# Talking-heads attention and Fourier mixing on one core: the Fourier transform folded a second time, and the second pair of row groups laid out about row 224

## The chip, the cores and the metric

The kernel runs on one core of a Trainium2 chip. The core has TensorE (matrix products, called PE in the profile, with PEld for its weight loads), VectorE (DVE), ScalarE (ACT), GpSimd (POOL) and SyncE (SP, which here only issues transfers). All five run their own queues in order and meet at semaphores. The metric is the device time of one execution in microseconds; several executions are timed and the median is given.

## What is computed

The reference joins two blocks. `x` is the attention result with its heads side by side, and it feeds a Fourier mixing layer with a feed-forward part. All numbers are fp32 (the two feed-forward weights come as 64-bit floats).

```python
batch, n_heads, seq, head_dim = (8, 12, 448, 64)
scores = scale * np.matmul(q, k.transpose(0, 1, 3, 2))
scores = np.einsum('bhij,hg->bgij', scores, w_pre)        # pre-mix of the heads
attn = softmax(scores)
attn = np.einsum('bhij,hg->bgij', attn, w_post)           # post-mix
x = np.matmul(attn, v)                                    # to (8, 448, 768)

X = np.fft.fft(x, axis=1)
X = np.fft.fft(X, axis=2)
u = x + np.real(X)
un = (u - mean(u)) / np.sqrt(var(u) + 1e-06)
out = u + np.maximum(un @ w_ch1, 0.0) @ w_ch2             # 768 -> 3072 -> 768
```

The real part of the two-dimensional transform is a sum of two products: cosines along the rows times cosines along the columns, less sines times sines. Cosines are even and sines odd, so rows `s` and `448 - s` may be added (or subtracted) before the product with cosines (or sines), and columns `d` and `768 - d` likewise. That is a fold: half as many rows and columns go into the products.

## The kernel before, in words

There are two phases. `mix_phase` does attention and the Fourier transform and leaves `u` in DRAM (`u_scr`). `ffn_phase` reads it and does the normalization and the feed-forward part. The change touches only the first.

**Steps.** The first phase runs through 192 steps, 24 for each of 8 batches, and is written as a software pipeline in one loop. A step handles 10 query rows of all heads twice over. Its stages lie in different steps: at step `s` the gather (`emit_gather`, SP) collects the scores of step `s + 4`; the pre-mix (`emit_premix`, L425, TensorE), the row maximum (`emit_max`, L433, DVE), the exponential (`emit_exp`, L441, ScalarE) and the scaling by the reciprocal sum (`emit_scale`, L449 and L450 on DVE, L452 on GpSimd) belong to step `s + 2`; the post-mix (`emit_postmix`, L462, TensorE) and the 32x32 transposes of its result (`emit_turn`, L473, DVE) belong to step `s`. The pre-mix writes the PSUM tile `mx`, of which there is one; the post-mix writes `po`, also one.

**Other work.** Between these stages work of four kinds is taken from lists by due time, counted in steps from the batch's first: score matmuls (`emit_qk`, L399, due times `AT_QK`), products of attention and values (`emit_av`, L489, `AT_AV`), transposes of q and k (`emit_xpose`, L376, `AT_T`), and the Fourier part below. Their results lie in four PSUM tiles (`pms`, tile `ms`). Their evictions from PSUM (`copy`, L285) wait in a list, `pend`, and are emitted by `flush`; the table `ENG` says which go to ScalarE ("a") and which to DVE ("d"). One operation on the feed-forward weights (`wts.deal(1)`) is added to DVE in each step.

**Row groups.** A batch's 448 rows form four groups of 112. Groups 0 and 1 hold rows 0 to 111 and their mirror images 447 down to 337, stored in reverse with one zero row. Groups 2 and 3 hold rows 112 to 224 and their mirror images 336 down to 225. `emit_av` writes a group transposed into `XT`; in a backward group (`back`) it writes with a negative step, and a memset (L513) clears the row without a partner. `emit_x` (L525, due at `AT_X`) transposes it to `X` (rows on partitions). After each second group `fold` puts six GpSimd operations into a list: sums of the two groups in two halves (L547), the fold of the columns (L551, L552), differences in two halves (L547) and their fold (L557). They give `xe` (385 columns) and `xo` (383). One of them is emitted in each step.

**Transform.** `emit_z` (L570, `AT_Z`) multiplies 97 to 128 columns of `xe` (or `xo`) of both row pairs with the row table `ts` (225 frequencies) and gives one of seven tiles `z`. `emit_s2` (L584, `AT_S`) multiplies the four even (or three odd) `z` with the column tables `tce` or `tdo` (385 frequencies), for one pair of row groups at a time. DVE adds the result to `X` and its mirror image (L595, L597). Then the rows go to `u_scr`: the forward group by SP (L610, and L612 for row 224), the backward group by an indirect transfer that GpSimd issues (L604).

**Order.** The order of TensorE, DVE and ScalarE is the order written in the loop (`manual_schedule`). The order of GpSimd's and SP's queues is set by the framework's scheduler when the program is built.

Of the kernel before, what the change touches and what calls it, by code (L numbers as in the profile page):

```python
# [16 lines left out]
P = 128  # L17
# [10 lines left out]

R = 5
# [9 lines left out]
PR = (GR, GR + 1)  # L39
XW = GR + 12  # L40
# [11 lines left out]

SH = S // 2
DH = DM // 2
EVEN = [(0, 97), (97, 96), (193, 96), (289, 96)]
ODD = [(0, 128), (128, 128), (256, 127)]
# [6 lines left out]
AT_T = ((7, 0), (18, 18), (15, 17))  # L63
AT_QK = ((0, 2, 2), (0, 1, 2), (0, 1, 2), (0, 1, 2),
         (0, 1, 2), (1, 1, 2), (0, 1, 2), (0, 1, 2))
AT_AV = ((0, 2, 4), (0, 1, 4), (3, 4, 5), (2, 3, 4))
AT_X = (11, 20, 25, 29)
AT_Z = (38, 38, 38, 38, 42, 42, 42)
AT_S = ((41, 44), (49, 53))

ENG = {("tr", "q", 4): "d", ("tr", "q", 3): "a", ("tr", "k", 4): "a",
       ("tr", "k", 3): "d", "QK": "aa", "AV": "aa", "X": "aa", "z": "a"}

# [9 lines left out]
def _consts():  # L83
    s = np.arange(S)
    ang = 2.0 * np.pi * (np.outer(s, np.arange(SH + 1)) % S) / S
    ts = np.zeros((GR + 1, 2, 2, SH + 1))
    for n in range(2):
        for x, fn in enumerate((np.cos, np.sin)):
            ts[:PR[n], n, x] = fn(ang[n * GR:n * GR + PR[n]])
    d = np.arange(DH + 1)  # L90
    ang = 2.0 * np.pi * (np.outer(d, d) % DM) / DM
    tc = np.zeros((P, len(EVEN), DH + 1))
    for n, (d0, w) in enumerate(EVEN):
        tc[:w, n] = np.cos(ang[d0:d0 + w])
    td = np.zeros((P, len(ODD), DH + 1))
    for n, (d0, w) in enumerate(ODD):
        td[:w, n] = np.sin(ang[d0 + 1:d0 + 1 + w])
# [3 lines left out]
    for x in range(2):  # L101
        for r in range(R):
# [4 lines left out]
    at = S - GR * np.arange(2) - np.arange(GR)[:, None]  # L107
    return {"at": at.astype(np.uint32), "ts": ts.astype(np.float32),
            "tc": tc.astype(np.float32), "td": td.astype(np.float32),
            "mk": mk.astype(np.float32)}  # L110
# [142 lines left out]
def mix_phase(ctx, tc, ident, q, k, v, w_pre, w_post, u_scr, wts):  # L253
# [19 lines left out]
    pxf = pool("pxf", 2)  # L273
# [49 lines left out]
    rows = cst.tile([GR, 2], U32, name="rows")  # L323
    ts = cst.tile([GR + 1, 2, 2, SH + 1], F32, name="ts")
    tce = cst.tile([P, len(EVEN), DH + 1], F32, name="tce")
    tdo = cst.tile([P, len(ODD), DH + 1], F32, name="tdo")

    def emit_tables():
        for t, n in ((rows, "at"), (ts, "ts"), (tce, "tc"), (tdo, "td")):
            nc.sync.dma_start(out=t, in_=cn[n].ap())  # L330
        return []
# [343 lines left out]
    with tc.manual_schedule(engines={ET.PE, ET.DVE, ET.Activation}):  # L675
        while s < TOT or any(fill.values()):
# [5 lines left out]
            if 0 <= s + LM < TOT:  # L682
                emit_exp(s + LM)
# [306 lines left out]
```

## Time and profile before

| What | Value |
|---|---|
| Median of three executions | 2539.23 us (2535.92 to 2539.9) |
| Profiled execution | 2539.07 us, span 2537.3 us |
| Mean granted TensorE clock | 0.989 |
| Busy: PE, DVE, ACT, POOL | 95%, 59%, 31%, 27% of the span |
| Last post-mix to first feed-forward matmul | 905.65 to 964.10 us |
| A batch in the steady stretch (first `z` to first `z`) | 107.9 to 110.4 us |

The first phase takes the first 15 of the 40 slices of the page. There the other engines are busier than the shares of the whole span say: from 542.81 to 651.50 us DVE works 82.7 of 108.7 us, ScalarE 70.6 and GpSimd 68.6. In lines of the timeline the first number is the start and the second the time to the last end, in microseconds; the bracket tells how long the engine was idle before and what it waited for. Consecutive matmuls overlap, so the pace is read from start to start.

### The profile page before, as it was taken

Reading aid. Unit: us, or ns where it says so; the run is one execution under the profiler, and the core shown is the slowest. Engines: PE = TensorE matmul, PEld = TensorE weight load, DVE = VectorE, ACT = ScalarE, POOL = GpSimd, SP = SyncE. Lnnn points to the kernel's source line nnn. Section 1 sums busy time; section 2 is a strip of 40 time slices with the busy share of each in tenths; the row PEclk is TensorE's granted clock in tenths of the full one; section 3 lists DMA queues with packets and bytes.
Section 4 is the critical chain, followed back from the end, with each engine's and each line's share of the span. In section 5 each row is a group of like instructions: output and inputs, shape, how many; then the busy total and the mean of one; then the engine's idle time right before and its main releaser. Section 6 shows DMA issues by size and latency. Waiting matters only on the chain.

```text
span 2537.3 us, 47605 instructions
## 1 busy us (share of the span) xinstructions
PE 2418.7 (95%) x18544; PEld 1555.7 (61%) x18544; DVE 1503.3 (59%) x3075; ACT 794.5 (31%) x2084; POOL 689.7 (27%) x1029
## 2 busy tenths in 40 slices
PE   4899999999999977989999999999999999999999
PEld 2344444444444445767777777777777777777776
DVE  1777767777776636677366646664666466633333
ACT  2666666666666623222211011101111111111110
POOL 5575665667554433232100000000000000000000
PEclk9999999999999988999999999999999999999999
DMA  5454545545553448233544444444444444443431
GB/s 156 142 171 156 162 157 154 178 159 171 165 156 135 136 156 279 81 134 116 194 137 150 141 153 137 151 139 155 135 151 138 155 135 152 126 154 118 131 112 50
DMA packets 154911, 373.01 MB, mean 147 GB/s; under 512 B 22471, under 2 KB 75719, under 8 KB 154688
## 3 DMA queue, kind: packets, MB, share of 16 engines
q1 hardware_dynamic: 123360, 260.63, 31.2%
q0 software_dynamic: 31328, 109.34, 14.7%
q8 instruction: 148, 2.42, 0.4%
q14 instruction: 75, 0.61, 0.1%
HBM read 212.96 MB, written 74.34 MB: 113 GB/s over the span
## 4 chain that ended last, share of the span: by engine, by line
PE 84%; DVE 5%; POOL 3%; DMA 3%; ACT 3%; issue 1%; SPq 1%; ACTq 0%; POOLq 0%; DVEq 0%
PE psP L833 17%; PE psP L887 17%; PE psR L833 9%; PE psR L887 8%; PE mx L425 5%; PE ms L489 5%; PE psQ L887 4%; PE psQ L833 4%; PE po L462 4%; PE ms L399 4%; PE ms L584 3%; DVE nmx L433 2%; ACT PP L441 2%; DMA Kr<-Sb 2%; PE ms L570 2%; POOL xs L547 1%
## 5 line engine op out<-in xcount | busy, mean ns | idle before, releaser
L887 PE MATMUL psP<-w2t,h 128*128 128x384 f32 x1344 | 468.8, 493 | 16.0 <-DVE u L893 16.0
L833 PE MATMUL psP<-ub,w1t 128*128 128x256 f32 x2016 | 463.4, 379 | 0.0
L833 PEld LDWEIGHTS psP<-ub,w1t 128*128 128x128 f32 x2016 | 383.4, 190 | 61.2 <-issue 0.8
L887 PEld LDWEIGHTS psP<-w2t,h 128*128 128x128 f32 x1344 | 257.5, 193 | 186.9 <-DVE u L893 19.0
L182 POOL DMA_DIRECT2D raw<-in_moe_w_ch_dram x120 | 70.0, 584 | 936.3 <-DVE tmp L221 902.3
L441 ACT ACTIVATE PP<-mx,nmx 128x448 f32<-128x448 f32 x384 | 240.3, 630 | 261.3 <-DVE nmx L433 226.2
L433 DVE TENSOR_REDUCE nmx<-mx 128x1 f32<-128x448 f32 x384 | 221.7, 619 | 166.7 <-PE mx L425 166.3
L452 POOL TENSOR_SCALAR PP<-PP,rcp 128x448 f32<-128x448 f32 x384 | 240.6, 637 | 285.5 <-DVE rcp L450 228.7
L893 DVE TENSOR_TENSOR u<-u,psP 128x384 f32<-128x384 f32 x336 | 183.8, 552 | 149.7 <-PE psP L887 147.6
L838 ACT COPY h<-psP 128x512 f32<-128x512 f32 x42 | 24.6, 586 | 786.8 <-PE psP L833 786.8
L833 PE MATMUL psR<-ub,w1t 128*128 128x256 f32 x1008 | 231.4, 379 | 0.8 <-POOL ub L813 0.8
L887 PE MATMUL psR<-w2t,h 128*128 128x384 f32 x672 | 230.5, 486 | 0.0
L425 PE MATMUL mx<-Kr,kw 60*64 60x448 f32 x1536 | 195.1, 551 | 31.9 <-ACT PP L441 17.4
L844 DVE TENSOR_TENSOR h<-h,psQ 128x512 f32<-128x512 f32 x42 | 28.9, 688 | 320.6 <-PE psQ L833 320.6
L473 DVE STREAM_TRANSPOSE Pv<-po 128x896 f32<-128x896 f32 x192 | 212.3, 1106 | 8.7 <-PE po L462 8.6
L833 PEld LDWEIGHTS psR<-ub,w1t 128*128 128x128 f32 x1008 | 191.4, 190 | 27.2 <-POOL ub L813 1.2
L462 PE MATMUL po<-PP,kw 60*32 60x448 f32 x3072 | 188.9, 548 | 13.2 <-POOL PP L452 9.4
L399 PE MATMUL ms<-kT,qT 64*60 64x448 f32 (+1 forms) x1536 | 186.7, 557 | 7.8 <-DVE kT L285 7.8
L285 ACT COPY Sb<-ms 124x448 f32<-124x448 f32 x384 | 184.3, 541 | 7.6 <-PE ms L399 5.2
L489 PEld LDWEIGHTS ms<-Pv,vv 64*64 64x64 f32 x5376 | 143.3, 133 | 68.4 <-issue 26.5
L887 PEld LDWEIGHTS psR<-w2t,h 128*128 128x128 f32 x672 | 127.2, 190 | 87.4
L489 PE MATMUL ms<-Pv,vv 64*64 64x120 f32 x5376 | 165.7, 268 | 0.0
(92 smaller groups left out, 2687.3 us busy)
## 6 DMA issues: line engine op xcount, KB each, us to landing
ub<-ub SPq DMA_DIRECT2D x294, 384.0 KB
Kr<-Sb SPq DMA_DIRECT2D x768, 105.0 KB
raw<-in_moe_w_ch_dram POOLq DMA_DIRECT2D x72, 256.0 KB, 3.2
raw<-in_moe_w_ch_dram POOLq DMA_DIRECT2D x48, 384.0 KB, 3.9
w<-wst POOLq DMA_DIRECT2D x18, 896.0 KB, 4.7
w<-wst POOLq DMA_DIRECT2D x12, 1344.0 KB, 5.8
w1t<-w SPq DMA_DIRECT2D x42, 384.0 KB
w2t<-w SPq DMA_DIRECT2D x42, 384.0 KB
```

The lines of the kernel that those rows point to most:

```text
L285: (nc.scalar.copy if eng == "a" else nc.vector.tensor_copy)(out=out, in_=in_)
L399: nc.tensor.matmul(pss[x][64 * y:64 * y + r0 + 64 - lo, :S], st["qT", xx][64 * x:64 * x + 64, y, lo:r0 + 64], st["kT", xx][64 * x:64 * x + ...
L425: nc.tensor.matmul(mx[64 * z:64 * z + 64, x, :S], kw1[64 * x:64 * x + KR, :], Kr[64 * x:64 * x + KR, z, :], start=True, stop=True)
L433: nc.vector.tensor_reduce(nmx[:, x:x + 1], steps[T]["mx"][:, x, :S], axis=AX.X, op=ALU.max, negate=True)
L441: nc.scalar.activation(PP[:, x, :], steps[T]["mx"][:, x, :S], ACTF.Exp, bias=steps[T]["nmx"][:, x:x + 1], accum_out=den[:, x:x + 1])
L452: nc.gpsimd.tensor_scalar(PP[:, x, :], PP[:, x, :], rcp[:, x:x + 1], 1.0, op0=ALU.mult, op1=ALU.mult)
L462: nc.tensor.matmul(po[o:o + 32, z, :S], kw2[64 * z:64 * z + KR, y, :], PP[64 * z:64 * z + KR, :, c * HS:(c + 1) * HS], start=True, stop=True)
L473: nc.vector.transpose(g["Pv"][:, T % GT, :].rearrange("p (z s) -> p z s", z=2), steps[T]["po"][:, :, :S])
L489: nc.tensor.matmul(pss[y][64 * x:64 * x + 64, :nu * R], st["v", pr][64 * y:64 * y + 64, x, jb * D:(jb + 1) * D], _ap(Pv, 64 * y * rp + 32 ...
L833: nc.tensor.matmul(p[:, m, :], w1[i][:, kc, m * P:(m + 1) * P], ub[:, kc, :], start=i in OPENS and m == kc == 0, stop=kc == NK - 1, skip_g ...
L887: nc.tensor.matmul(p, lhs[i][:, kf, x * P:(x + 1) * P], w2[i][:, kf, :], start=i in OPENS and kf == 0, stop=kf == FM - 1, skip_group_check ...
L893: nc.vector.tensor_tensor(us_, us_, p, op=ALU.add)
```

## The change

The transform is folded a second time. In the rows, even and odd frequencies are kept apart: for even frequencies rows `p` and `224 - p` may be added, for odd ones subtracted (for sines the other way round). For that the second pair of row groups is laid out about row 224: group 2 holds rows 224 down to 112 and group 3 rows 224 up to 336, so that both pairs have 113 rows `p` = 0 to 112, and pair 0 and pair 1 are added and subtracted partition by partition. In the columns, `d` and `384 - d` are folded in the same way.

- `fold` puts eight more operations into the list after the second pair: `both` (sum and difference of the two pairs, for `xe` and for `xo`) and `again` (the column fold: a sum, a difference, and a copy of the middle column). Two entries of the list are emitted in each step.
- `emit_z` makes four double tiles in place of seven: each of its four matmuls has one parity of the columns and of the rows. Frequencies of one parity lie two apart in PSUM, so that the output has a step of two. The rows of `z` are ordered so that `emit_s2` finds those of a pair side by side.
- `emit_s2` has four matmuls for each row pair and parity, two for each parity of the column frequencies, again with an output step of two.
- The tables `ts` and `tcs` are smaller; `tce` and `tdo` are gone.
- The backward group of pair 0 and the forward-named group of pair 1 are scattered by GpSimd; the others go by SP in one transfer each.
- `ENG`, the due times and the order of the stages in a step differ: the maximum comes after `flush`, the exponential after the value products, the score matmuls before `emit_turn`, the gather before the scaling.

```diff
-EVEN = [(0, 97), (97, 96), (193, 96), (289, 96)]
-ODD = [(0, 128), (128, 128), (256, 127)]
+PLACE = ((0, 1, (GR,)), (GR - 1, -1, (0, GR)), (GR, -1, ()), (1, 1, (0,)))
+DQ = DH // 2
+CW = DQ // 2 + 1
+FOLD = (((CW, CW - 1), (CW - 1, CW - 1)), ((CW - 1, CW - 1), (CW - 1, CW - 2)))
-AT_T = ((7, 0), (18, 18), (15, 17))
-AT_QK = ((0, 2, 2), (0, 1, 2), (0, 1, 2), (0, 1, 2),
-         (0, 1, 2), (1, 1, 2), (0, 1, 2), (0, 1, 2))
-AT_AV = ((0, 2, 4), (0, 1, 4), (3, 4, 5), (2, 3, 4))
-AT_X = (11, 20, 25, 29)
-AT_Z = (38, 38, 38, 38, 42, 42, 42)
-AT_S = ((41, 44), (49, 53))
-ENG = {("tr", "q", 4): "d", ("tr", "q", 3): "a", ("tr", "k", 4): "a",
-       ("tr", "k", 3): "d", "QK": "aa", "AV": "aa", "X": "aa", "z": "a"}
+AT_T = ((-4, 1), (18, 14), (15, 17))
+AT_QK = ((0, 2, 3), (1, 1, 2), (0, 1, 2), (0, 1, 2),
+         (1, 2, 2), (0, 1, 2), (0, 1, 2), (0, 2, 2))
+AT_AV = ((0, 3, 4), (0, 1, 4), (3, 4, 5), (2, 3, 4))
+AT_X = (11, 19, 24, 29)
+AT_Z = (39, 39, 42, 42)
+AT_S = ((41, 44), (53, 56))
+ENG = {("tr", "q", 4): "a", ("tr", "q", 3): "a", ("tr", "k", 4): "a",
+       ("tr", "k", 3): "a", "QK": "aa", "AV": "dd", "X": "aa", "z": "d"}
...
+        def both(par, op):
+            nm, w = ("xe", "xo")[par], DH + 1 - 2 * par
+            box.append(pxs.tile([PN, DM], F32, name="xs", tag="xs")[:, :w])
+            pl.tensor_tensor(box[-1], st[nm, 0][:, :], st[nm, 1][:, :], op=op)
+        def again(par, r):
+            if r == 0:
+                st["xf", par] = pxf.tile([PN, 2, 2, DQ + 1], F32, name="xf",
+                                         tag=f"xf{par}")
+            x, t = st["xf", par][:, r], box[-1]
+            n, w = DQ - par, DH + 1 - 2 * par
+            for y, op in enumerate((ALU.add, ALU.subtract)):
+                pl.tensor_tensor(x[:, y, :n], t[:, :n], t[:, w - 1:w - 1 - n:-1], op=op)
+            pl.tensor_copy(out=x[:, 0, n:n + 1], in_=t[:, n:n + 1])
...
+        if pair:
+            for par in range(2):
+                for r, op in enumerate((ALU.add, ALU.subtract)):
+                    folds.extend([lambda par=par, op=op: both(par, op),
+                                  lambda par=par, r=r: again(par, r)])
...
-        ps = ms_tile()
-        for pair, n in enumerate(PR):
-            nc.tensor.matmul(ps[:w, :SH + 1],
-                             batches[b]["xf", pair][par][:n, d0:d0 + w],
-                             ts[:n, pair, par, :], start=(pair == 0), stop=(pair == 1))
+        w, at = FOLD[par][y]
+        ps = ms_tile().rearrange("p (n q) -> p n q", n=2)
+        for n, d0 in enumerate((0, at)):
+            for r in range(2):
+                k = GR if par ^ r else PN
+                nc.tensor.matmul(ps[:w, n, r:SH + 1:2],
+                                 batches[b]["xf", par][:k, par ^ r, y, d0:d0 + w],
+                                 ts[:k, par, r, :PN - r], start=True, stop=True)
...
-        for ch, (_, w) in enumerate(chunks):
-            nc.tensor.matmul(ps[:n, :DH + 1], st["z", par, ch][:, i0:i0 + n],
-                             tab[:w, ch, :],
-                             start=(ch == 0), stop=(ch == len(chunks) - 1))
+        for y in range(2):
+            w, _ = FOLD[par][par ^ y]
+            for ch in range(2):
+                nc.tensor.matmul(ps[:n, y:DH + 1:2],
+                                 st["z", par, par ^ y][:w, ch, i0:i0 + n],
+                                 tcs[:w, par, y, ch, :DQ + 1 - y],
+                                 start=(ch == 0), stop=(ch == 1))
...
                 emit_premix(s + LM)
-                emit_max(s + LM)
             flush()
             if 0 <= s + LM < TOT:
-                emit_exp(s + LM)
+                emit_max(s + LM)
             if 0 <= s < TOT:
                 emit_postmix(s)
             take("AV", s)
+            if 0 <= s + LM < TOT:
+                emit_exp(s + LM)
+            take("QK", s)
             if 0 <= s < TOT:
                 emit_turn(s)
             if s >= 4:
                 wts.deal(1)
-            if 0 <= s + LM < TOT:
-                emit_scale(s + LM)
-            if folds:
-                folds.pop(0)()
-            take("QK", s)
             if 0 <= s + LG < TOT:
                 if any(e[2] is not None and e[2] <= (s + LG) // BS for e in pend):
                     flush()
                 emit_gather(s + LG)
+            if 0 <= s + LM < TOT:
+                emit_scale(s + LM)
+            for _ in range(min(2, len(folds))):
+                folds.pop(0)()
             take("full", s)
```

## The prediction

> **What bounds the kernel now.** I read the page first, then the order of time on TensorE and on GpSimd in a batch of the steady stretch, then the waits. The slices and the chain:
>
> ```profile
> PE   4899999999999977989999999999999999999999
> POOL 5575665667554433232100000000000000000000
> PE 84%; DVE 5%; POOL 3%; DMA 3%; ACT 3%; issue 1%; SPq 1%; ACTq 0%; POOLq 0%; DVEq 0%
> ```
>
> TensorE sets the time almost everywhere; the change lies in the first 15 slices (the mixing, 0 to about 964 us). The next lines are one batch: the first transform (L570), the second (L584), a step that another wait ends, and the post-mix that GpSimd delays.
>
> ```profile
> 542.74 3.29 PE L570 MATMUL ms<-ts,xe 112*97 112x225 f32 x16
> 545.96 0.98 PE L425 MATMUL mx<-Kr,kw 60*64 60x448 f32 x8
> ...
> 595.15 2.85 PE L584 MATMUL ms<-tce,z 97*113 97x385 f32 x8
> 597.84 0.82 PE L525 MATMUL ms<-ident,XT 128*113 128x128 f32 x6
> ...
> 616.29 0.98 PE L425 MATMUL mx<-Kr,kw 60*64 60x448 f32 x8
> ...
> 625.82 0.99 PE L462 MATMUL po<-PP,kw 60*32 60x448 f32 x16 [0.69 <-POOL PP L452]
> ...
> 640.44 0.98 PE L425 MATMUL mx<-Kr,kw 60*64 60x448 f32 x8 [0.21 <-ACT PP L441]
> ```
>
> Read start to start, not durations: 16 first-transform instructions take 3.22 us (0.201 each), 8 second-transform ones 2.69 (0.336). The last line is the floor of a step: pre-mix, maximum, exponential and the next pre-mix share one PSUM tile, so a step with little TensorE work still lasts 3.81 us (636.63 to 640.44).
>
> GpSimd in the same batch, around the last X of the batch:
>
> ```profile
> 615.18 1.25 POOL L452 TENSOR_SCALAR PP<-PP,rcp 128x448 f32<-128x448 f32 x2 [1.69 <-DVE rcp L450]
> 616.63 1.97 POOL L547 TENSOR_TENSOR xs<-X 113x384 f32<-113x384 f32 x2 [0.20 <-ACT X L285]
> 618.66 0.19 POOL L551 COPY xe<-xs 113x2 f32<-113x2 f32 x1
> 618.93 1.00 POOL L552 TENSOR_TENSOR xe<-xs 113x383 f32<-113x383 f32 x1
> 620.01 2.17 POOL L547 TENSOR_TENSOR xs<-X 113x384 f32<-113x384 f32 x2
> 622.25 1.00 POOL L557 TENSOR_TENSOR xo<-xs 113x383 f32<-113x383 f32 x1
> 623.42 1.05 POOL L604 DMA_INDIRECT u<-X,rows  x1 [0.16 <-issue]
> 624.51 1.26 POOL L452 TENSOR_SCALAR PP<-PP,rcp 128x448 f32<-128x448 f32 x2
> ```
>
> The fold is one unbroken block of 6.62 us (8 with the scatter), and the scaling that post-mix needs stands behind it in GpSimd's queue. It ends at 625.77; post-mix, ready at 625.05, waits. Over 216 to 865 us TensorE's waits for this add up to 8.2 us in six batches, 1.37 each.
>
> **The change part by part.** Steps are numbered 0 to 23 within a batch of 24.
>
> *Matmuls.* Each fp32 matmul is two instructions. The first transform goes from 28 instructions of 225 columns to 32 of 112 or 113; the second from 28 of 385 to 32 of 192 or 193. A line through the two paces (0.201 at 225, 0.336 at 385) is 0.84 ns a column plus 0.011 us: 113 columns 0.106, 193 columns 0.173. First: 28 x 0.201 - 32 x 0.106 = 2.24. Second: 28 x 0.336 - 32 x 0.173 = 3.87. Together 6.1 us a batch. Weight loads stay hidden: seven 128-wide transposes (L376, 565.14 to 566.00) go at 0.123 each with a 128-wide load behind each; were 0.123 the floor for the 97-wide ones as well, 32 x 0.017 = 0.5 a batch would be lost. Outside the tail lie seven first transforms and first row pairs (2.24 + 1.93 each) and six second pairs (1.93): **-40.8 us**, by the load bound -37.
>
> The outputs now step by two elements in PSUM; no matmul of the trace writes with a step. The nearest row, post-value L489, reads its moving operand in runs of five at full pace (56 in 1.49 us over four quadrants), but writes unbroken. Bounds: no cost, or a write per column at half pace, the old 0.201 and 0.336 or so: 32 x 0.095 + 32 x 0.163 = 8.3 a batch, +60. I take none, since an fp32 column already takes 0.84 ns. The Trainium skill speaks against it (PSUM — Partial Sum Buffer, Specifications (TRN2)): lines are 8 bytes, and any access that is not contiguous slows matmuls significantly. It names no factor, and no run here shows one; by the rule the sum would stand above mine by some part of that bound.
>
> *GpSimd, second fold.* Four full-width sums (383 to 385) at 1.00 plus 0.08 to the next, eight of 192, four one-element copies at 0.19. A 192-wide sum is bounded by half of L552 (0.50) and by the line from the four-element L787 (0.274) to 383 (1.00), 0.64; I take 0.58. Full sum, two halves and copy: 1.08 + 1.16 + 0.22 = 2.46, four times 9.8 us a batch. GpSimd is 63% busy in the batch from 542.81 (68.6 of 108.7), so it has room on average. But two folds a step are only the order written; the queue order of the built program is another. In batches 3, 5 and 6, and nearly so in 1, 2 and 4:
>
> ```
> scale(7) | pair sums, xe, xo | both, again | both, again | both |
> scale(8) | again | both, again | scale(9) | scale(10)
> ```
>
> scale(8) now stands behind 6.62 + 0.08 + 2 x 2.46 + 1.08 = 12.7 us. Let t6 be the pre-mix start of step 6. Scale(7) ran 4.42 after the pre-mix start of its step before (610.76 to 615.18); step 5 shrinks to some 4.0 (post-mix, second transform, X), so it ends at t6 + 1.6 and the block starts there. Scale(8) ends at t6 + 1.6 + 12.7 + 1.25 = 15.6. Its post-mix could start at t6 + 4.1 (step 6, as 616.29 to 620.39) + 3.8 (step 7, at the floor) + 0.9 = 8.8: **a stall of 6.8**. TensorE's queue is in order; values, scores, second transforms and the next pre-mix wait behind that post-mix, and the transpose on DVE, exponential and gathers behind those. Post-mix 9 follows 4.2 later, at 19.7; scale(9) ends at 15.6 + 3.85 + 1.25 = 20.7: 0.9 more. The earlier block (first row pair) has no second fold; with a load of k (2.9) and the scatter (1.05) before the scaling after it, I count 0.3. So 8.0 a batch; 0.5 more in batch 0, where scale(9) has more ahead of it, and 0.6 in two where a weight load (L182) cuts in: 57.7 for seven, less 9.6 of now: **+48**. With 0.50 for halves, the block starting at t6 + 0.4 and steps a little longer it is 5.0 a batch (+26); with 0.64 and weight loads, 8.8 (+52).
>
> *Evictions and order.* Values and z go from ScalarE to DVE, transposes from DVE to ScalarE. The four copies of a value step (0.21 each on ScalarE, 0.17 to 0.30 on DVE by its smallest and small operations) run between the reciprocals and the maximum, while pre-mix takes 1.13; they fit or miss by 0.3. The maximum now stands behind evictions: in step 9 behind four X additions (1.9), ready 1.0 late, under the stall of scale(9). ScalarE's q transposes (about 2.0) fit the 2.4 between exponentials. Scores ahead of the transpose and the gather ahead of the scaling change no wait that TensorE sees; gather of block 0 has about 1 us to spare. Four memsets for two (0.11) and one row transfer fewer on SP are under 0.2. Step floor: by my count of each step's work, steps 0, 1, 7, 11, 14 and 19 fall below 3.8 and lose 1.4 a batch, a q transpose waited for 0.6; now it is 0.75 for the exponential and 1.0 for kT: **+2** in all (-5 to +8).
>
> *Head.* Tables fall from 1.79 to 0.80 MB; at the 160 GB/s of the first 50 us that is up to 6 us before the gather for which pre-mix waits until 48.64. Half: **-3** (-6 to 0).
>
> *Tail.* Now from the last fold's start (921.18) to the last addition (943.68): 22.5 us. After: block 6.62, scatter 1.04, two second folds 4.9 = 12.6, even transform and eviction 3.2, its second transform 2.1; odd ready at 17.5; then 2.5 + 0.8, three second transforms 6.3, additions 2.1, some 29.6, at a clock between half and full. Ahead of it 4.5 are gained (fewer second transforms before the last X, and less than the 3.64 wait of the last post-mix): **+2.5** (-3 to +8).
>
> Sum, against the profiled run's 2539.07 (span 2537.3 and 1.8 around it; 0.2 under the median): 2539.1 - 40.8 + 48 + 2 - 3 + 2.5 = **2548**. The feed-forward stretch behind 964 us is untouched.
>
> **The rivals.**
> 1. *The second fold stays covered* (other side: faster). TensorE keeps its gain if scale(8) ends by t6 + 8.8; each us by which it is late costs 7. For: 37% of GpSimd idle, a slack of about 3 us now. Against: a 6.62 us block already causes waits. Without added waits: 2539.1 - 40.8 + 1.5 = 2500; with half of them 2524.
> 2. *Strided PSUM writes are slow* (slower): 2548 + 60 = 2608 by the bound, 2578 at half. For: no row shows such a write. Against: the fp32 pace.
> 3. *The tail takes it*: at half clock throughout, second transforms at 2.8 and halves at 0.64, +8 to +15: 2554 to 2561.
> 4. *It doesn't halve the work*: instructions grow from 56 to 64, so a fixed cost per matmul above my 0.011 would eat it; at the 0.123 floor 2552.
>
> **How the numbers follow.** Mine has 0.60, own range 2522 to 2560 (the bounds of the stalls, -22 to +4, and of floor and tail). Rival 1 has 0.20, rival 2 0.10, rivals 3 and 4 together 0.10. A measurement tells 0.2%, 5 us, from no change. Mine gives 0.15 faster, 0.09 same, 0.36 slower; rival 1 0.20 faster; rival 2 0.10 slower; the last two 0.02 same, 0.08 slower: faster 0.35, same 0.11, slower 0.54. The range 2505 to 2575 takes in most of rival 1 and some of rival 2.
>
> **What would show it.** L570 and L584 at about 0.106 and 0.173 start to start (twice that: rival 2). Once a batch a block of some 12.7 us on GpSimd and behind it a post-mix waiting 5 to 7 us for PP, summing to 35 to 60 us; below 20, rival 1. A batch of 108 to 110 us, as now; 102 would prove me wrong. Wrong also if the maximum waits for DVE's evictions in ordinary steps.

## The result, and the profile after

The changed kernel takes 2688.61 us (median; 2687.75 to 2692.73) beside 2537.57 us (2534.55 to 2539.9) for the kernel before on the same chip: 1.0599 times as long, 95% interval 1.0581 to 1.0618, or 151 us slower. The prediction of 2548 us had the sign and missed the size; its range ended at 2575. The profiled execution took 2688.28 us (span 2686.5).

The slices of the page, with the clock that TensorE was granted:

```profile
PE   3898888999798986489899999999999999999999
POOL 4476756565665444232310000000000000000000
PEclk7998998898898988799999999999999999999999
```

and the clock of the kernel before:

```profile
PEclk9999999999999988999999999999999999999999
```

The dips lie almost all in the first 17 slices, the mixing. The granted clock is below nine tenths in ten of them, and in two of the kernel before. (The chain of waits that the page follows back from the end accounts for some 60% of the span, TensorE 56%; it breaks off at the tail and says nothing about the mixing.) The rest of the extra time is found by stretches: the first pre-mix starts at 61.34 us (before 48.64), from there to the start of the last post-mix instruction it is 970.7 us (before 857.5), from there to the first load of `u` 63.7 us (before 39.9), and from there to the end 1591 us in both. So +12.7, +113 and +24.

Two lines of TensorE's timeline answer to the transform lines of before, the first transform in the steady stretch and the second in the tail's last 24:

```profile
998.11 1.79 PE L601 MATMUL ms<-ts,xf 113*97 113x113 f32 x16
1000.08 0.98 PE L436 MATMUL mx<-Kr,kw 60*64 60x448 f32 x8 [0.17 <-ACT PP L452]
...
1063.53 4.18 PE L616 MATMUL ms<-tcs,z 96*112 96x193 f32 x24 [1.12 <-DVE z L297]
```

Sixteen first-transform instructions take 1.8 us (before 3.3) and 24 second-transform ones 4.2, 0.174 each (before 0.336). From start to start, where no wait follows, 16 instructions take 1.63 us (245.21 to 246.84) and eight 1.40 (255.81 to 257.21): 0.102 and 0.175 each, where 0.106 and 0.173 were predicted. The outputs' step of two in PSUM costs nothing that can be seen.

The block of GpSimd and the post-mix behind it, with TensorE's own lines between (timeline of both engines):

```profile
436.91 1.25 POOL L463 TENSOR_SCALAR PP<-PP,rcp 128x448 f32<-128x448 f32 x2 [2.52 <-ACT X L297]
438.13 1.95 POOL L554 TENSOR_TENSOR xs<-X 113x384 f32<-113x384 f32 x2
...
445.75 1.14 POOL L579 TENSOR_TENSOR xf<-xs 113x192 f32<-113x192 f32 x2
446.11 0.98 PE L436 MATMUL mx<-Kr,kw 60*64 60x448 f32 x8 [0.70 <-ACT PP L452]
...
451.09 1.26 POOL L463 TENSOR_SCALAR PP<-PP,rcp 128x448 f32<-128x448 f32 x2
...
452.40 1.75 PE L473 MATMUL po<-PP,kw 60*32 60x448 f32 x16 [5.31 <-POOL PP L463]
454.08 1.77 PE L410 MATMUL ms<-kT,qT 64*64 64x448 f32 x8
```

The block lasts 13.0 us (438.13 to 451.09; predicted 12.7) and post-mix waits 5.31 (predicted 6.8). But behind the wait everything takes nearly twice its time: 16 post-mix instructions 1.75 us in place of 0.98, eight score matmuls 1.77. The busy times of the ten microseconds behind the wait show why (columns: length, then PE, PEld, DVE, ACT and POOL, granted clock, DMA share, GB/s):

```profile
452.00:457.00 5.00, 4.60 (x28) 1.73 (x29) 2.04 (x4) 0.97 (x2) 4.84 (x10) 0.50 0.23 89
457.00:462.00 5.00, 5.00 (x32) 1.66 (x30) 3.02 (x6) 0.15 (x1) 3.49 (x4) 0.50 0.17 55
```

TensorE was granted half its clock. The prediction priced the wait and not this.

What it had not seen at all is in the waits. SyncE's queue, ScalarE and TensorE, the lines that are new or larger:

```profile
SPq L642 <- DMA u<-X,rows: 149.5, 8, 26.6
ACT X L297 <- DMA u<-X,rows: 43.8, 6, 8.4
PE mx L436 <- DMA Kr<-Sb: 37.9, 18, 25.7
PE po L473 <- POOL PP L463: 37.5, 11, 5.8
PE ms L410 <- ACT X L297: 31.1, 6, 6.2
```

The columns are the total in us, how often, and the longest. In the kernel before the first wait was 6.7 us, once, the third 12.4 and the fourth 9.4; the second and the last did not occur. SyncE's direct write (L642) now waits for GpSimd's scatter in every batch, up to 26.6 us, and the eviction of `X` waits for the same scatter, which still reads the buffer. One such place:

```profile
479.93 0.31 SPq L642 DMA_DIRECT2D u<-X  x1
479.96 0.86 ACT L297 COPY X<-ms 113x384 f32<-113x384 f32 x2 [7.04 <-DMA u<-X,rows]
480.35 19.81 SPq L426 DMA_DIRECT2D Kr<-Sb  x19
...
480.49 2.14 PE L410 MATMUL ms<-kT,qT 64*64 64x448 f32 x8 [4.85 <-ACT X L297]
...
483.08 4.78 PE L436 MATMUL mx<-Kr,kw 60*64 60x448 f32 x8 [0.45 <-DMA Kr<-Sb]
```

ScalarE was idle for 7.04 us, TensorE for 4.85; the gathers that had queued behind SyncE's write then go out in one row of 19, and a pre-mix that takes 0.98 us lasts 4.78.

The scatter's own rows tell why. The line of the scatter, from issue to landing, after (before 3.5, 3.6 and 8.5 us); the landing is given for six of the 16 only:

```profile
L636 POOL DMA_INDIRECT u<-X,rows x16: 991/1718/2505, 279.6 to 1076.7; - x16
DMA to landing us min/median/max: 3.5/5.4/19.6
```

In the tail two scatters stand apart. The first pair's 112 rows move 0.34 MB within 3.5 us. The second pair's 113 rows are issued at 1076.65 and land 18.6 us later. Up to 1085 us the page counts 870 packets under 512 B; then rows alone go. The transfers from 1085 to 1090 us:

```profile
DMA packets 22, 0.14 MB, mean 27 GB/s; under 512 B 0, under 2 KB 0, under 8 KB 22
q0 software_dynamic: 22, 0.14, 6.4%
```

The last figure is the share of 16 engines' time. One of sixteen, busy throughout, is 6.25%: the figure is that of a scatter that goes through one DMA engine. The Trainium skill (DMA: Bandwidth & Descriptors, the section on why a DMA increments its semaphore by 16) says that the engines used are the largest number up to 16 that divides the slowest dimension of both sides (it excepts some direct copies that GpSimd issues; the scatter is an indirect one). 113 is a prime, 97 too, and 112 is 7 times 16. Rows and rule agree, in the scatter as in the table of 97 rows. From 55 to 60 us, while the first pre-mix is still waited for, the only transfer on the core's DMA engines is one of packets of some 6 KB, the length of a row of the column table:

```profile
DMA packets 21, 0.13 MB, mean 26 GB/s; under 512 B 0, under 2 KB 0, under 8 KB 21
q1 hardware_dynamic: 21, 0.13, 6.3%
```

SyncE's gathers wait 10.0 us for that table in the head.

### The profile page after: what moved, and what is told of

It is laid out like the page before. It is cut to its first block, busy times and chain, and to the rows that moved or that the text cites. A ratio compares the mean times of both kernels' runs of the same rounds, so it can differ in the third digit from the quotient of the medians.

```text
span 2686.5 us, 47832 instructions
## 1 busy us (share of the span) xinstructions
PE 2456.4 (91%) x18608; PEld 1570.4 (58%) x18608; DVE 1557.0 (58%) x3443; ACT 753.2 (28%) x1692; POOL 772.5 (29%) x1173
## 2 busy tenths in 40 slices
DMA packets 161477, 372.09 MB, mean 139 GB/s; under 512 B 29258, under 2 KB 82619, under 8 KB 161252
## 4 chain that ended last, share of the span: by engine, by line
PE 56%; DVE 2%; DMA 1%; ACT 0%; issue 0%; POOL 0%; SPq 0%; POOLq 0%; DVEq 0%
PE psP L865 16%; PE psP L919 16%; PE psR L865 8%; PE psR L919 8%; PE psQ L919 4%; PE psQ L865 4%; DMA u<-X,rows 1%; PE psQ L837 1%; DVE wst L225 0%; DVE tmp L233 0%; DVE wst L237 0%; DVE tmp L229 0%; DMA u<-u 0%; DVE u L925 0%; ACT ub L839 0%
## 5 line engine op out<-in xcount | busy, mean ns | idle before, releaser
L436 PE MATMUL mx<-Kr,kw 60*64 60x448 f32 x1536 | 237.0, 575 | 65.5 <-DMA Kr<-Sb 37.9
L410 PE MATMUL ms<-kT,qT 64*64 64x448 f32 (+1 forms) x1536 | 208.3, 586 | 33.2 <-ACT X L297 31.1
L473 PE MATMUL po<-PP,kw 60*32 60x448 f32 x3072 | 200.7, 581 | 37.5 <-POOL PP L463 37.5
L500 PEld LDWEIGHTS ms<-Pv,vv 64*64 64x64 f32 x5376 | 149.3, 137 | 75.1 <-issue 46.4
L500 PE MATMUL ms<-Pv,vv 64*64 64x120 f32 x5376 | 172.2, 275 | 0.0
```

What stands on the lines that cost most here:

```text
L410: nc.tensor.matmul(pss[x][64 * y:64 * y + r0 + 64 - lo, :S], st["qT", xx][64 * x:64 * x + 64, y, lo:r0 + 64], st["kT", xx][64 * x:64 * x + ...
L436: nc.tensor.matmul(mx[64 * z:64 * z + 64, x, :S], kw1[64 * x:64 * x + KR, :], Kr[64 * x:64 * x + KR, z, :], start=True, stop=True)
L473: nc.tensor.matmul(po[o:o + 32, z, :S], kw2[64 * z:64 * z + KR, y, :], PP[64 * z:64 * z + KR, :, c * HS:(c + 1) * HS], start=True, stop=True)
L500: nc.tensor.matmul(pss[y][64 * x:64 * x + 64, :nu * R], st["v", pr][64 * y:64 * y + 64, x, jb * D:(jb + 1) * D], _ap(Pv, 64 * y * rp + 32 ...
```

## Experiments

Three theories. S: the 113-row scatter (and the 97-row table) goes through one engine and what waits for it costs. P: GpSimd's second fold costs. R: the evictions that moved and the order of the stages cost. Times are medians, set against runs of the kernel before on the same chip (2537 to 2541 us).

### The scatter and the table

*Scatter of 112 rows*, the 113th row by SyncE:

```diff
-    ap=rows[:n, pair:pair + 1], axis=0), in_=X[:n, :], in_offset=None)
+    ap=rows[:GR, pair:pair + 1], axis=0), in_=X[:GR, :], in_offset=None)
+if n > GR:
+    nc.sync.dma_start(out=u_scr[b][SH - GR:SH - GR + 1, :], in_=X[GR:n, :])
```

> The second row pair's scatter takes 112 rows (as the first pair's, and as both in the kernel before); the 113th row, row 224, is written by SP. What is computed is the same. Theory S (in the changed kernel the 113-row scatter lands in 19.6 us where the 112-row one lands in 3.5; SP's direct write of the other group waits for it with the gathers behind it, and the X buffer comes free late): every scatter lands in under 5 us, the direct write L642 no longer waits (now 149.5 us over 8), nor the eviction of X (43.8 us over 6), the batch shrinks from 125 to 110-115 us, and the time falls by 85 to 115 us to 2575-2605. Theory P (what costs is GpSimd's second fold ahead of the scaling, 37.5 us of post-mix waiting, and TensorE's clock after such gaps): the waits on the scatter go away, but others take their place; the time falls by no more than 30 us. Theory R (the evictions moved to DVE and the other order of the stages): likewise within 30 us of 2688.

2602.42 us, ratio 1.0249 (1.0232 to 1.0266): 86 us less, as S expected, and out of reach for P and R. The landing is given for two scatters only, both of the first pair, and stays at 5.5 us:

```profile
DMA to landing us min/median/max: 5.4/5.5/5.5
```

For the second pair's scatter the waits tell: the eviction's is gone, its issue takes about 1.05 us in place of 2.49, and SyncE's for the scatter falls from 149.5 to 26.4 us (now for the single row).

*Column table of 112 rows* (`np.zeros((CW, ...` and the tile `tcs` with `GR` in place of `CW`):

> The column table has 112 rows, the last 15 zero and unused, in place of 97; nothing else differs. If the table's 97-row load is what delays the first pre-mix (61.34 us, before 48.64), because it goes through one DMA engine: the load spreads over the engines, the first pre-mix starts at 46 to 51 us and the time falls by 10 to 14 us. If the head is late for another reason (the queues' order): the first pre-mix stays at 59 to 63 us, and the time within 3 us.

2673.05 us, ratio 1.053 (1.0513 to 1.0548): 15.5 us less. The first pre-mix starts at 39.4 us, 22 earlier, and even 9 earlier than in the kernel before (whose row table has 113 rows too, of twice the length; whether that is the reason wasn't tried). Some of it is lost again before the mixing is steady.

*Both together:*

> The scatter of 112 rows (row 224's partner, the 113th, by SP) and the column table of 112 rows together. If the two are independent, their gains add up: 86 us (2688.6 to 2602.4) and 15.5 us, so 2587 (2582 to 2592). What then remains above the kernel before, some 46 us, would by theory P be GpSimd's second fold. If the table's gain is lost once the scatters are quick, or the other way round: 2595 to 2603.

2584.89 us, ratio 1.0173 (1.0156 to 1.019): the gains add up, to 103.7 us. This is called the repaired kernel below.

*Direct write first*, the scatter still of 113 rows:

```diff
-            for back in range(2):
+            for back in ((0, 1), (1, 0))[pair]:
```

> The loop over the two groups of the second pair runs the other way: the direct write by SP is issued ahead of the 113-row scatter. The scatter still has 113 rows and lands in some 19 us. If what costs is the SP queue held by the direct write (and gathers behind it: pre-mix waiting 37.9 + 32 us for Kr): L642 waits under 30 us in all, and the time falls by 60 to 100 us; the X buffer's wait (43.8 us) may stay. If what costs is the X buffer that comes free late: the fall is 20 to 40 us. By theory P or R: under 15 us.

2663.11 us, ratio 1.0492 (1.0469 to 1.0514): only 25.5 us less. My account of the scatter was wrong in one part. SyncE's wait for the scatter falls to 14.1 us (another 19.5 stand in the tail, at the first load of `u`) and the wait of `X` vanishes, yet 60 of the 86 us stay. Pre-mix now waits longer for the gathers. From the timeline, with SyncE's queue free and the scatter issued at 460.33:

```profile
472.28 0.93 PE L436 MATMUL mx<-Kr,kw 60*64 60x448 f32 x2 [1.19 <-DMA Kr<-Sb]
476.25 1.76 PE L436 MATMUL mx<-Kr,kw 60*64 60x448 f32 x4 [3.03 <-DMA Kr<-Sb]
478.26 1.75 PE L436 MATMUL mx<-Kr,kw 60*64 60x448 f32 x2 [0.26 <-DMA Kr<-Sb]
```

In all pre-mix waits 57.4 us for `Kr` (37.9 in the changed kernel). While the scatter runs, the gathers are in flight beside it and late. Of the cost, most stays with the scatter itself, whichever queue is held. That the gathers are late at the one engine that it keeps busy fits the share of one in sixteen; these views don't show single engines.

*The kernel before with a 113-row scatter*, everything else as it was:

```diff
-    at = S - GR * np.arange(2) - np.arange(GR)[:, None]
+    at = S - GR * np.arange(2) - np.arange(GR + 1)[:, None]
+    at[GR] = S
...
-    ap=rows[:GR, pair:pair + 1], axis=0), in_=X[:GR, :], in_offset=None)
+    ap=rows[:n, pair:pair + 1], axis=0), in_=X[:n, :], in_offset=None)
```

> The kernel before, with one thing of the change alone: its second pair's scatter has 113 rows (the 113th, a row without content, goes to the spare row behind the last). Its direct write already stands ahead of the scatter. Theory S: this scatter lands in 15 to 20 us where it took 3.7; X or the next direct write waits for it, and the time rises by 10 to 50 us, with the head and the GpSimd stall as in the kernel before. Theories P and R: the time stays within 5 us of the kernel before.

2609.0 us, ratio 1.027 (1.0251 to 1.0289): one row more in eight transfers costs 68 us, more than I had expected, with none of the fold. The waits of the weight loads of pre-mix for the gathers were 18.6 us in 15 places before, 11.7 of it in the head. Now:

```profile
DMA to landing us min/median/max: 3.5/11.8/26.1
PEld mx L426 <- DMA Kr<-Sb: 52.5, 34, 12.0
```

Here the landing is given for every scatter: 19.5 to 26.1 us for the eight of 113 rows, 3.5 to 4.0 for those of 112. The gathers are not the whole cost: post-mix waits 21.6 us for the scaling (9.4 before), which stands behind a scatter whose issue now takes 2.5 us in GpSimd's queue in place of 1.05.

### The second fold on GpSimd

*The kernel before with the second fold's GpSimd work alone*, its result unread:

```diff
+        if pair:
+            for par, (a, b) in enumerate(zip(batches[g["b"]]["xf", 0], (xe, xo))):
+                for op in (ALU.add, ALU.subtract):
+                    folds.extend([lambda a=a, b=b, op=op: both(a, b, op),
+                                  lambda par=par: again(par)])
...
-            if folds:
+            for _ in range(min(2, len(folds))):
```

> The kernel before and the second fold's GpSimd work alone: four sums of 385 or 383 columns, eight halves of 192 and four copies of one element behind the second pair's fold, two list entries a step, with a result that nothing reads. No matmul is saved and no transfer differs; GpSimd's queue then stands as in the changed kernel, the scaling behind 12.7 us of fold. My prediction's term for this was +48 us by the length of the stalls alone (57.7 less 9.6). Theory with the clock: a stall of 5.3 to 6.8 us once a batch, and 4 to 5 us a batch for TensorE at half clock behind it, +65 to +85 us, 2605-2625. Stalls alone: +28 to +48 us, 2569-2589. If the scaling's delay is hidden: within 10 us of the kernel before.

2601.34 us, ratio 1.0237 (1.0219 to 1.0255): 60 us, more than the stalls alone (28 to 48) and a little less than the theory with the clock (65 to 85). One block, from TensorE's timeline:

```profile
549.79 1.75 PE L462 MATMUL po<-PP,kw 60*32 60x448 f32 x16 [6.90 <-POOL PP L452]
551.47 2.84 PE L489 MATMUL ms<-Pv,vv 64*64 64x120 f32 x56
...
554.99 0.98 PE L462 MATMUL po<-PP,kw 60*32 60x448 f32 x16
```

and the busy times of that stretch (the last three columns: granted clock, share of the DMA engines, GB/s):

```profile
545.00:550.00 5.00, 0.21 (x8) 0.21 (x16) 0.18 (x1) 0.65 (x3) 4.64 (x8) 0.71 0.50 166
550.00:555.00 5.00, 5.00 (x81) 2.84 (x69) 2.06 (x4) 0.58 (x4) 4.68 (x10) 0.61 0.17 56
555.00:560.00 5.00, 4.61 (x64) 1.14 (x64) 4.21 (x8) 3.23 (x9) 4.93 (x8) 1.00 0.54 143
```

TensorE waits 6.90 us and then runs at half clock for some 4 us. Post-mix's waits for the scaling are 57.1 us in all, 9.4 before: 47.7 by length, as much as the prediction had (+48). The other 12.6 us I put down to the slow clock: TensorE's other waits add up to what they were, and the same 18544 instructions keep it busy for 2432.7 us in place of 2418.7. The Trainium skill (TensorE: Matmul & The Clock Gate, Part 1) puts half clock down to idle gaps longer than about 3.4 us; the gaps in the two places shown are 5.3 and 6.9 us, which agrees.

*GpSimd's queue in the written order* in the repaired kernel, in the changed one alone, and in the kernel before as a control:

```diff
-    with tc.manual_schedule(engines={ET.PE, ET.DVE, ET.Activation}):
+    with tc.manual_schedule(engines={ET.PE, ET.DVE, ET.Activation, ET.Pool}):
```

> The two repairs together, and GpSimd's queue in the order written in the loop (each scaling ahead of the next two folds) in place of the framework's. Theory P, as now refined: of the 46 us that the repaired kernel lies above the one before, a post-mix that waits 5.3 us for the scaling once a batch (37.2 us in all) is one part, and TensorE's clock at 0.50 for some 10 us behind it another, some 4 to 5 us a batch. Both go: the wait of L473 for PP falls below 15 us, the granted clock of the mixing returns to 0.99 or more, and the time falls by 55 to 75 us below the kernel with both repairs, to 2512-2532, faster than the kernel before. If only the wait itself counts: 2548 to 2556. If the waits for the scaling move to another place (the evictions on DVE, a scatter that waits in GpSimd's queue): 2565 or more.

> The changed kernel with GpSimd's queue in the written order and nothing else: scatter and table keep 113 and 97 rows. Theory: what the second fold costs on GpSimd (37.5 us of waiting and the clock behind it) and what the scatter costs (86 us) are separate, so the time falls by 40 to 75 us, to 2614-2648, with the scatter's waits as they were. If the scatter's waits hide behind the fold's stall, or the scatter now holds up the scalings in the written order: 2670 or more.

> The kernel before with GpSimd's queue in the written order, as a control: its waits for the scaling are 9.4 us in all, with no clock lost behind them. The time falls by 0 to 10 us, to 2528-2541. The fold's own worth, apart from the order of the queue, is then the distance from this kernel to the repaired one in the same order: by my matmul terms some 20 to 35 us. If the written order is worth more here (20 us or more), the second fold's gain is smaller than it looks.

2586.25 us (ratio 1.0177, 1.016 to 1.0194), 2672.5 (1.0508, 1.049 to 1.0525) and 2601.82 (1.0241, 1.0224 to 1.0258). None did what I had hoped for. In the repaired kernel the wait for the scaling does shrink, from 39.0 to 4.4 us, but another takes its place:

```profile
PE ms L533 <- POOL XT L522: 42.8, 8, 6.9
...
PE po L473 <- POOL PP L463: 4.4, 4, 1.2
```

A memset of a few columns, which a transpose needs, stands behind two entries of the fold. And the written order alone costs the kernel before 61 us, where a scaling stands behind loads and scatters that GpSimd issues: post-mix waits 29.6 us for it (9.4 before), which is a part of the 61.

*The memset on DVE* besides (`nc.vector.memset` at L522):

> Both repairs and GpSimd's queue in the written order, and besides the memset of XT's row without a partner on DVE, behind the copies into the same tile, in place of GpSimd, where it stood behind two entries of the second fold (a transpose that waits 42.8 us over 8 for it, 6.9 at most, took the place of the post-mix's 39.0 us over 10). Refined theory P: a stall of some 5.4 us a batch costs its length and, with TensorE's clock at 0.50 for 10 us behind it, 4 to 5 us more. So without the memset's stall the time falls by 50 to 70 us, to 2516-2536, faster than the kernel before. If the clock plays no part: 2545 to 2553. If the waits find a third place: 2565 or more.

2566.49 us, ratio 1.0095 (1.0073 to 1.0117): 20 us less, a third of what I had expected; post-mix waits 21.7 us again. In each of these orders something urgent still stood behind the fold.

*Without the second fold's operations*, all matmuls, evictions and transfers as in the repaired kernel (the first transform reads tiles that were folded once only, so what comes out is not the reference's):

```diff
-    batches[b]["xf", par][:k, par ^ r, y, d0:d0 + w],
+    batches[b][("xe", "xo")[par], par ^ r][:k, d0:d0 + w],
...
-        if pair:
-            for par in range(2):
-                for r, op in enumerate((ALU.add, ALU.subtract)):
-                    folds.extend([lambda par=par, op=op: both(par, op),
-                                  lambda par=par, r=r: again(par, r)])
```

> The kernel with both repairs, without the second fold's GpSimd operations; the first transform reads 97 (96) columns of xe and xo in place of the twice folded tiles, so what it transforms is not the reference's, and all matmuls, evictions and transfers are as in the repaired kernel. It prices the rest of the change without that block. My terms: matmuls -40.8, evictions and order +2, with a head of -9 and a tail of +3 as now measured: 2541 less 45 is 2496 (2488 to 2504). By the batches of the repaired kernel, where step 8 with the stall is 7.0 us longer than before and the other 23 steps together only 1.5 us shorter, most of the matmuls' gain is lost outside the stall: 2585 less 7 x 7.0 and what half clock costs behind it, 2518 to 2536.

2515.53 us, ratio 0.9904 (0.9885 to 0.9922). In the repaired kernel the fold on GpSimd thus costs 69 us, and all the rest of the change is worth 25 us, not 45. By the two profiles (67 us apart) post-mix waits 39.0 us for the scaling with the fold and 2.1 without, the first transform in the tail 10.0 and 2.1 for its operand, and TensorE is busy 21.4 us longer with the same instructions. Of the 25 us 7.7 lie in the head, where the table of 112 rows helps, 12 in the mixing and 5 in the tail.

*The second fold on DVE* (`both` and `again` with `nc.vector`, one entry a step):

```diff
+            later.extend([lambda: None] * 4)
...
+            if later:
+                later.pop(0)()
```

> The kernel with both repairs, and the second fold (sums, halves and copies) on DVE, one list entry a step from four steps after the last X, in place of GpSimd. GpSimd's block is again the 6.6 us of the first fold. DVE gets some 5 us more a batch, spread over eight steps (385 columns take 0.55 there, as the additions to X). If the stall is the block's length and DVE has the room (87 of 113 us busy): the post-mix waits under 12 us in all for PP, TensorE's granted clock goes back to 0.99, the fall is 45 to 60 us, to 2525-2540: at or below the kernel before. If the maximum is delayed by DVE's extra work instead: 2550 to 2575. If DVE and GpSimd get in each other's way: above 2575.

2528.32 us, ratio 0.9948 (0.9928 to 0.9968): 12 us or half a per cent below the kernel before. The post-mix waits 4.1 us in all, and in the stretch of one batch and a bit the clock is full, with DVE 85% busy (columns as above):

```profile
466.00:574.00 108.00, 104.22 (x1587) 50.78 (x1586) 91.84 (x229) 65.37 (x164) 69.68 (x110) 1.00 0.55 169
```

### Where the matmuls' gain stays

The mean length of a step over five steady batches, from one pre-mix start to the next (some of the 24 steps, and their sum, us):

| Kernel | step 1 | 8 | 9 | 12 | 13 | 14 | 16 | 17 | all 24 |
|---|---|---|---|---|---|---|---|---|---|
| before | 6.23 | 4.13 | 3.75 | 4.10 | 4.05 | 5.98 | 4.15 | 6.24 | 108.7 |
| changed | 3.79 | 10.42 | 4.83 | 12.52 | 8.64 | 3.75 | 5.02 | 5.44 | 126.0 |
| repaired | 3.79 | 11.17 | 4.83 | 4.09 | 4.01 | 3.95 | 5.02 | 5.74 | 114.2 |
| no second fold | 3.79 | 4.23 | 4.63 | 4.10 | 4.01 | 3.92 | 5.03 | 5.35 | 106.1 |
| fold on DVE | 3.81 | 4.23 | 4.63 | 4.10 | 4.02 | 4.18 | 5.03 | 5.34 | 106.7 |

Step 8 is the fold's stall, steps 12 and 13 the scatter. Without both the batch is 2.6 us shorter than before, where the matmuls save 6.1. Steps 1 and 14 gave up the transform's work and stand at 3.8 to 4.2, about the floor. By their size the waits of pre-mix's weight loads account for about the rest: without the second fold 75.4 us for the exponential (before 65.9), 23.5 for the gathers (before 6.9 without the head), together 26 us in some 7.5 batches. Three parts were undone to find what makes the gathers late.

*SyncE's writes ahead of the scatter* (the loop of the direct-first run, and the single row ahead of the scatter), with the fold on DVE and without the fold; *the evictions as before* (`ENG` of the kernel before); *the due times as before* (`AT_T`, `AT_QK`, `AT_AV`), without the fold and with it on DVE:

> The second fold on DVE and both repairs, with the second pair's writes in another order: SP's direct write and the single row first, the 112-row scatter last, so that SP no longer waits for a scatter (in the repaired kernels 26.4 us over 7, with gathers behind it). If that wait is where part of the matmuls' gain goes (pre-mix's loads wait 25.4 us for Kr, 18.6 before of which 11.7 in the head): the batch loses 0.8 to 1.6 us and the time falls by 6 to 12 us, to 2516-2522. If gathers are late for another reason: within 4 us of 2528.

> The kernel with both repairs and without the second fold's operations (the first transform reads xe and xo, so its result is not the reference's), with SP's writes ahead of the scatter. If SP's wait was the artefact of my repair: 6 to 12 us below the 2515.5 of the same kernel with the scatter first, 2503-2510, and the batch at 104.5 to 105.3; my matmul term (-6.1 a batch) is then mostly seen. If the batch stays at 106.1: the steps' floor has taken the rest.

> As the run with the single row first, but with the evictions on the engines of the kernel before: values and z on ScalarE, q's and k's outer transposes on DVE. DVE then has 90.9 us a batch less some 10. If the evictions on DVE delay the maximum and so hold steps at the floor (pre-mix waiting for the exponential: 32.1 + 83.0 us, before 17.4 + 65.9): the time falls by 5 to 12 us below that run. My prediction held the move to be nearly free: within 4 us. If ScalarE is then too late for the exponential: 5 to 15 us more.

> As the run without the second fold and with SP's writes first (the first transform reads xe and xo, so its result is not the reference's), and with the due times of transposes, scores and values of the kernel before. Pre-mix's weight loads wait 22 us for Kr there and 75 for the exponential, 6.9 (without the head) and 65.9 before. If the change's due times make the gathers late: the wait for Kr falls under 12 us and the time by 6 to 15 us, to 2502-2511. If the shorter steps do (SP issues four gathers a step at 0.77 us each, 3.1 of the 3.8 us of a step at the floor): within 4 us of 2517, or longer, as the old due times were laid for other steps of the transform.

> As the run with the evictions of the kernel before (second fold on DVE, single row first), and with its due times of transposes, scores and values as well: of the change only the fold itself, the layout, the transform's due times and the order of the stages are left. If the due times cost: 2508 to 2517. If not: within 4 us of 2522, or longer.

| Run | us | Ratio to the kernel before (95%) |
|---|---|---|
| writes first, fold on DVE | 2526.79 | 0.9951 (0.9938 to 0.9963) |
| writes first, no second fold | 2517.19 | 0.9919 (0.9896 to 0.9941) |
| writes first, fold on DVE, evictions as before | 2522.46 | 0.9943 (0.9928 to 0.9958) |
| writes first, no second fold, due times as before | 2524.45 | 0.9935 (0.9917 to 0.9954) |
| as the third, due times as before | 2527.3 | 0.9937 (0.9922 to 0.9953) |

None differs from its partner by more than the intervals: not the single row, not the evictions, not the due times. The waits do differ in one case. Without the second fold and with SyncE's writes first, pre-mix's weight loads wait as in the first two lines; with the due times of before besides, as in the last two:

```profile
PEld mx L436 <- ACT PP L452: 74.9, 120, 2.8
PEld mx L436 <- DMA Kr<-Sb: 22.1, 33, 1.8
...
PEld mx L436 <- ACT PP L452: 95.7, 120, 2.8
PEld mx L436 <- DMA Kr<-Sb: 8.1, 13, 1.7
```

With the fold on DVE it is the same (gathers 23.8 to 10.8, exponential 76.8 to 92.8). So it was mostly the new due times that made the gathers late, and what is won there is waited for at the exponential instead. Of theory R the evictions and these three due times are out as causes of a longer time. The order of the stages in a step and the transform's own due times were not undone; whether the missing 20 us (25 in place of 45) lie there or at the floor of a step stays open. The version with the fold on DVE, SyncE's writes first and the evictions as before has the lowest median of those that compute the whole result, 0.6% below the kernel before; the four with the fold on DVE can't be told apart.

## Why the prediction was wrong

- **Matmuls, -40.8.** The paces were right to 0.004 us, and rival 2 (slow strided writes, +60 by its bound) is refuted: the rule of the Trainium skill (PSUM — Partial Sum Buffer, Specifications (TRN2)) that accesses that aren't contiguous slow matmuls doesn't show in these fp32 matmuls, and the measurement decides. What failed is that a saved microsecond of TensorE is a saved microsecond of the batch. From the first pre-mix to the last post-mix the kernel without the second fold takes 845.5 us, before 857.5: 12 us, where -40.8 and +2 for order and floor were predicted. The rest, some 3.5 a batch, is about what the waits for the exponential and for the gathers grew by; what keeps them there isn't shown. Rival 4 (a fixed cost for each matmul) is refuted by the paces as well.
- **GpSimd's second fold, +48.** The mechanism and its place were right: the block is 13.0 us long (12.7 predicted) and post-mix waits behind it. That the lengths add up to 47.7 us in the kernel before is in part luck, since in the changed kernel they are 37.5, 28 above before, with 5.3 us in place of 6.8 in the stall shown: the lower bound of the term (+26). What the term left out is the half clock behind each stall. In all the fold costs 60 us in the kernel before and 69 in the repaired one, tail included. Rival 1 was not what happened; with the fold on DVE the stalls are gone, yet the time is 2528 us and not rival 1's 2500.
- **Evictions and order, +2.** Undoing the evictions moves the time by less than can be told; that part of the term stands. The order of the stages was not undone. That no wait for the gathers would be seen ("gather of block 0 has about 1 us to spare") doesn't.
- **Head, -3 (-6 to 0).** It was +12.7 us. The step that failed is the rate: I took 160 GB/s for every table by its size; the 97-row table goes at 26 GB/s when it is alone, one engine's share. With 112 rows the first pre-mix comes 9 us earlier than before.
- **Tail, +2.5 (-3 to +8).** It was +24: 18 from the scatter, and +5.4 with 112 rows (45.3 against 39.9 us), within the bounds; rival 3 had the place and not the cause. In the changed kernel's tail the third write of SyncE and the loads of `u` stand behind the scatter:

```profile
1067.84 27.85 SPq L642 DMA_DIRECT2D u<-X  x3
...
1076.65 2.38 POOL L636 DMA_INDIRECT u<-X,rows  x1 [3.37 <-issue]
1095.74 5.51 SPq L788 DMA_DIRECT2D u<-u  x10
```

- **What the sum left out.** The scatter appeared with its issue time on GpSimd alone (1.05 us). That a transfer whose row count changes from 112 to 113 may land at another rate, and who waits for its landing, was not asked. This is the step that failed most: a term put at nothing that measures 86 us, 104 with the table's. It is not the only one: the repaired kernel's 2585 us still lie above the range, by the clock behind the stalls and the matmuls' lost gain.

Put together from the runs, each difference taken from the run before it: scatter and table +104, the fold on GpSimd +69, the rest of the change -25; that is 148 us, the distance to the kernel before in those runs (2540.7 us); the 151 us are measured from 2537.57.

## What to carry to other kernels

When an edit changes the shape of a transfer, price the landing and not only the issue, and look at what the row count does: 112 and 113 rows differ by 15 us here. Undoing a held queue need not give the time back, because other transfers in flight beside the slow one can be late too, as the gathers were here. A stall of 5 to 7 us on the engine that sets the time cost more than its length here, by a stretch at half clock behind it. Work put onto an engine that is idle a third of the time was not free, because something urgent stood behind it in that engine's queue. And a microsecond of TensorE that is saved in a step at its floor is not one saved in the time.

## What the runs showed of the hardware

- A scatter of 113 rows of 3 KB landed in 18.6 and 19.6 us in the changed kernel and in 19.5 to 26.1 in the kernel before with 113 rows, one of 112 rows in 3.5 to 5.6 (once 8.5). Its issue on GpSimd takes 2.4 to 2.5 us in place of 1.0, and the page counts some 850 more packets under 512 B for each: 29258 in place of 22426 over eight.
- fp32 matmuls that write PSUM with a step of two run at 0.102 us for 113 columns and 0.175 for 193, about the line through unbroken ones (0.201 at 225 and 0.336 at 385).
- Behind an idle gap of 5.3 us TensorE ran at a granted clock of 0.50 for some 10 us (452 to 462), and behind one of 6.9 us at half its pace for some 4.
